# Attention and a gated layer on one core: one left-over sum for two pairs, and another engine for the last piece of key weights

## The chip, the cores and the metric

The kernel runs on one core of one Trainium2 chip. The metric is the device time of one execution in microseconds, the median of several runs. The core has five engines that work from queues of their own: TensorE (PE, matmuls; its weight loads are PEld), VectorE (DVE), ScalarE (ACT), GpSimd (POOL) and SyncE (SP, which here only starts DMA transfers). Each works strictly in the order in which the program gave it its instructions.

## The reference, cut to what matters

```python
# q, k, v: (8 batches, 12 heads, 448 rows, 64)
scores = cap * np.tanh(scale * (q @ k.T) / cap)
attn = np.exp(scores - max); attn = attn / (attn.sum(-1) + 1e-9)
x = (attn @ v) as (8, 448, 768)
xk = mu_k * x + (1 - mu_k) * x_prev          # x_prev: x one row earlier
xr = mu_r * x + (1 - mu_r) * x_prev
k = np.maximum(xk @ w_k, 0)                   # 768 -> 1024
out = sigmoid(xr @ w_r) * (k * k @ w_v)
```

All is float32. Products that need more than one pass are made of a high and a low part of each operand. The weights come as float64 and are put together from their two 32-bit words on the chip.

## The kernel before, in words

**Pairs and steps.** The 8 x 12 heads are 48 pairs of two heads. `run` calls `step(i)` once per pair; each step is a string of operations written out by hand (lines 59 to 82), and `step` (L840) calls them one after the other. So the strings fix the order of the work on every engine. A number in a name is a group of keys: 448 keys are three groups of 128 (0, 1, 2) and 64 left-over keys. Group 3 holds the left-over keys of two pairs, i and i + 1, together: at even steps `S3` (scores), `tanh3` and `exp3` work on one tile of 128 x 2 x 448 for both pairs, whose index 1 is i % 2 (with the 128 partitions shared by two heads).

**The sums of a pair.** `red` (L345) sums exponentials over 32 keys at a time on VectorE with a transposing reduce. For groups 0 to 2 it reads 128 x 896 and writes 128 x 28; for group 3 it reads one pair's half of the tile, 128 x 448, and writes 128 x 14. So there is a `red3` at every step: at even steps behind `exp3`, near the step's end, and at odd steps ahead of the `f`s. The results lie in `r1` (L182), one for even and one for odd pairs, each the first row of a tile `sq_0` or `sq_1`. In the next step `gather` (L353) moves partitions 32 to 127 of `r1` to partitions 0 to 31 with three DMAs of SP's queue; `recip` (L357, four VectorE instructions) adds them up, inverts and transposes; `rec_store` writes the reciprocals to DRAM, and `rec_load` (L372, two DMAs on SP's queue) reads them back spread over 128 partitions as `r`. In the step after that `norm` (L381, VectorE) multiplies the pair's values, in PSUM as `pv`, by `r`. `mix_old` (L392, ACT) and `mix_new` (L394, VectorE) mix rows; `mix_new` is the last to read the pair's `pv` bank, of which there are two, and so lets `V`, the product of exponentials and values of a later pair (L314 and L340), begin. `x_high` and `x_low` (GpSimd) split the mixed rows.

**Key weights.** The pieces of w_k are made in steps 0 to 12: piece n is loaded in step n - 1, `weight_abs` takes its magnitude in step n, and five calls of `f` (`fill`, each one a step of the generator `weight_round`) do one VectorE instruction each (L577, L580, L582, L584, L586). `weight_sum` (L591) then adds the two words (L593), copies the sum as its high part to `wkh` (L122) and subtracts to get the low part `wkl` (L132), all three on GpSimd. Pieces 10 and 11 are halves, 384 columns wide, of the last 128 of the 1024 key columns. Piece 11 gets its five `f`s in step 12, and `weight_sum` follows in the same step. The matmuls with the key weights (`K`, six at a time here, L474) of step 12 are the last 18 of batch 0: they need both pieces, the last nine of them piece 11, and they stand one behind the other in PE's queue.

**Step 12.** Its string (`TURN[0]`, L80) is, with what each engine sees of it cut to this case:

```
... S0 S1 V S3 S2 f f f f f gate_new tanh0 exp0 red0 norm
weight_sum tanh1 exp1 K relu_early red1 tanh3 tanh2 qk_high ... mix_new recip ... qk_low x_high x_low ...
K red2 ... K relu k_store weight_abs exp3 red3 ... load_qk rec_load weight_store N0 N1
```

The `norm` of step 12 is that of pair 10, and its `r` is loaded behind the end of step 11. `qk_high` and `qk_low` are GpSimd work (L122, L132) on a later pair. From step 13 on the matmuls of the next batch (L498) fill PE; after step 47 the second half of the kernel multiplies by w_v and w_r (L711).

Of the kernel before, what the change touches and what calls it, by code (L numbers as in the profile page):

```python
# [10 lines left out]
F32 = mybir.dt.float32  # L11
F32R = mybir.dt.float32r
AF = mybir.ActivationFunctionType
ALU = mybir.AluOpType
# [15 lines left out]
P = 128  # L30
# [18 lines left out]
RM = 3 * NB  # L49
RC = RM + NB // 2  # L50
# [5 lines left out]

ODD = """load_v gather quad_load weight_load S0 S1 V S2 red3 f f f f f gate_new tanh0 exp0 red0
weight_sum tanh1 exp1 red1 norm recip x_store rec_store K qk_high qk_low tanh2 relu mix_old k_store prep mix_new x_high x_low gate_old  # L60
K exp2 red2 weight_rest weight_sum relu k_store prep K prep K relu k_store prep
weight_abs load_qk rec_load quad_load tail_open weight_store"""
EVEN = ODD.replace("V S2", "V S3 S2").replace(" red3", "").replace("tanh2", "tanh3 tanh2").replace("K relu k_store prep\n", "K exp3 red3 relu k_store prep\n")
ROWS = """gather weight_store load_v quad_load quad_load weight_load 135:U 3:turn PE 135:red3 f f f f f tanh0 exp0 0:turn 0:PE_TURN red0
weight_sum tanh1 15:PE_TURN exp1 23:relu red1 gate_new norm recip x_store 1:k_put rec_store 235:k_put qk_high qk_low 024:tanh3 tanh2 0234:exp2 4:turn mix_old mix_new x_high x_low gate_old
15:exp2 red2 weight_rest weight_sum 0:weight_abs 0:relu 024:exp3 024:red3 12345:weight_abs load_qk rec_load PE_END"""
ROWS_PE = (("VV S3 S2", "K18", "N0 N1"), ("K15", "S2 N0 turn K15", "N1"), ("WW K6 T S3 S2 K18", "", "N0 N1"),
# [1 line left out]
STEP_0 = """gather rec_load load_v x_store weight_load S0 S1 V0 S2 V1 S3 V2 V3 f f f f f tanh0 exp0 red0  # L69
weight_sum tanh1 exp1 weight_abs red1 recip rec_store qk_high qk_low tanh2 exp2 norm red2 tanh3 exp3 mix_old red3 mix_new x_high x_low  # L70
load_qk weight_store"""
ODD_6 = """load_v gather weight_load weight_low S0 S1 V S2 red3 f f f f f gate_new tanh0 exp0 red0 norm
weight_sum tanh1 exp1 K relu_early red1 tanh2 qk_rise relu exp2 mix_old k_store mix_new recip x_store rec_store qk_low x_high x_low gate_old
K red2 weight_rest weight_sum relu k_store K K weight_abs relu k_store load_qk rec_load weight_store"""
EVEN_6 = ODD_6.replace("V S2", "V S3 S2").replace(" red3", "").replace("tanh2 qk_rise", "tanh3 tanh2 qk_high").replace("weight_abs", "weight_abs exp3 red3")
STEP_6 = """gather rec_load load_v x_store weight_load weight_low S0 S1 V0 S2 V1 S3 V2 V3 f f f f f tanh0 exp0 red0
weight_sum tanh1 exp1 red1 recip rec_store tanh2 qk_rise exp2 norm red2 K qk_low weight_abs tanh3 exp3 mix_old red3 mix_new x_high x_low
load_qk rec_load"""
STEP_1 = STEP_0.replace("S3 ", "").replace("tanh3 exp3 mix_old red3", "mix_old").replace("f f f f f", "red3 f f f f f")
TURN = (EVEN_6.replace("K K weight_abs", "K relu k_store weight_abs") + " N0 N1",  # L80
        " ".join(x for x in ODD_6.replace("S0 S1 V S2", "U K15").replace("tanh1", "tanh1 S2 N0 turn K15").split() if x not in ("K", "relu", "relu_early", "k_store")) + " N1")
LAST = """gather f f f f VV recip rec_store norm rec_load K mix_old relu k_store prep mix_new x_high x_low gate_old
K gate_new relu k_store prep K prep K relu k_store prep x_store tail_open"""
# [4 lines left out]
def rows(phase):  # L88
    pe = dict(zip(("PE", "PE_TURN", "PE_END"), ROWS_PE[phase]))
    do = [x.split(":") for x in ROWS.split()]  # L90
    return " ".join(pe.get(x[-1], x[-1]) for x in do if len(x) == 1 or str(phase) in x[0])


def strings(i):
    if i < ALONE:
        return ((STEP_0, STEP_1) if i < 6 else (STEP_6, ODD_6))[i % 2]
    if i < REST[0]:
        return (TURN if i >= 12 else (EVEN_6, ODD_6))[i % 2]
    if i < NPAIR:
        return rows(i % NP)  # L100
    return ((LAST.replace("gather", "gather relu k_store"), LAST) if i < NPAIR + 2 else (EVEN, ODD))[i % 2]


def f(ap):
    return ap.bitcast(F32)


class Body:
# [73 lines left out]
    def init_sums(self, pool):  # L182


        nc = self.nc
        self.r1, self.sr, self.sq = [], [], []
        for j in range(2):
            t = pool.tile([P, 8, RC], F32, name=f"sq_{j}")
            self.r1.append(t[:, 0])
            self.sq.append(t[0:32])  # L190
            self.sr.append(pool.tile([32, 32], F32, name=f"sr_{j}"))
            nc.gpsimd.memset(self.sr[j], 1.0)

# [151 lines left out]
    def red(self, i, g):  # L345
        p32, r1 = self.P32[i, g], self.r1[i % 2]
        if g == 3:
            p32 = p32[:, i % 2:i % 2 + 1]
        self.nc.vector.tensor_reduce(out=r1[:, 0:RM].rearrange("p (x g) -> p x g", g=3)[:, :, g] if g < 3 else r1[:, RM:RC],  # L349
                                     in_=p32.rearrange("p h (b k) -> p (h b) k", k=32),  # L350
                                     axis=mybir.AxisListType.X, op=ALU.add, apply_transpose=True)

    def gather(self, i):  # L353
        for q in range(1, 4):
# [236 lines left out]
    def weight_sum(self, e="p"):  # L591
        for n, a, sq in self.w_sum:
            {"p": self.nc.gpsimd, "v": self.nc.vector}[e].tensor_add(sq, f(a), sq)  # L593
            cols = self.key_piece(n)
            if cols:
                c, d = cols
                hi, lo = (x[:, d[0]:d[-1] + 1, c * P:(c + 1) * P] for x in (self.WKH, self.WKL))
                sq = sq.rearrange("p (c n) -> p c n", n=P)
                self.copy(e, hi, sq)
                if len(d) < ND:  # L600
                    self.sub(e, lo, sq, f(hi))
                else:
                    self.w_low.append((lo, sq, hi))
            else:
                self.w_done.append((n, sq))
        self.w_sum = []

    def weight_low(self):
        for lo, sq, hi in self.w_low:
            self.sub("v", lo, sq, f(hi))  # L610
        self.w_low = []
# [469 lines left out]
```

## Time and profile before

| | |
|---|---|
| median of 3 runs | 889.12 us (887.44 to 890.73) |
| the profiled execution | 889.26 us, its span 887.4 us |
| PE busy | 862.9 us (97%) |
| DVE, ACT, POOL busy | 730.0, 624.8, 411.1 us |
| mean granted TensorE clock | 0.99 |

The span runs from the first to the last instruction; the 1.9 us between it and the execution's own time lie around it. PE's busy time is modelled, since matmuls overlap. In what follows a time such as 127.11 is in us from the start of the span.

### The profile page before, as it was taken

The page shows a single profiled execution, that of the slowest core. Times are in us where ns is not written, and L with a number is a line of the kernel's source. Part 1 is how long each engine was busy: PE and PEld are TensorE (multiplying, and loading weights), DVE is VectorE, ACT ScalarE, POOL GpSimd, SP SyncE. Part 2 cuts the span into 40 slices and gives each one's busy share as a digit, 9 for nine tenths or more (in the row PEclk, how much of TensorE's full clock was granted, in tenths as well). Part 3 has the DMA queues.
Part 4 walks back from the last instruction along what each step waited for, and adds up shares of the span by engine and source line. Part 5 has one row for each costly group of instructions (what it writes and reads, how often), then busy time and mean ns, then how long its engine had stood idle before and what let it go on. Part 6 is the DMA issues. An engine that isn't in the chain of part 4 may idle for free.

```text
span 887.4 us, 16618 instructions
## 1 busy us (share of the span) xinstructions
PE 862.9 (97%) x5826; PEld 707.7 (80%) x5826; DVE 730.0 (82%) x1246; ACT 624.8 (70%) x922; POOL 411.1 (46%) x346
## 2 busy tenths in 40 slices
PE   7789999999999999999999999999999999999996
PEld 3226667777766777777766899999999999999996
DVE  6988996999999999999879847888787667777775
ACT  8897888988888889888786655665656535555553
POOL 4996584777877777867754100000000033333430
PEclk9889999999999999999999999999999999999999
DMA  5575746577676667666665738554546546667763
GB/s 162 168 215 183 215 144 197 183 207 227 201 225 210 202 201 232 209 215 186 189 215 180 242 107 259 162 173 145 168 150 182 159 136 209 218 216 215 219 216 103
DMA packets 121374, 169.53 MB, mean 191 GB/s; under 512 B 20288, under 2 KB 105408, under 8 KB 121280
## 3 DMA queue, kind: packets, MB, share of 16 engines
q1 hardware_dynamic: 118544, 164.04, 59.5%
q10 hardware_dynamic: 2736, 4.33, 1.3%
q8 instruction: 48, 0.79, 0.4%
q14 instruction: 46, 0.38, 0.2%
HBM read 109.91 MB, written 56.60 MB: 188 GB/s over the span
## 4 chain that ended last, share of the span: by engine, by line
PE 88%; DVE 5%; ACT 1%; POOL 1%; DMA 1%; issue 1%; SPq 1%; ACTq 0%; DVEq 0%; POOLq 0%
PE ps L711 40%; PE kps L498 19%; PE pv L314 11%; PE s L277 9%; PE kps L474 4%; PE pv L340 2%; PE s L270 2%; DVE sq L349 2%; PE s L474 1%; ACT p L290 1%; ACT p L303 1%; DVE wa L582 0%; DVE xk L397 0%; DVE wa L580 0%; DMA sq<-sq 0%
## 5 line engine op out<-in xcount | busy, mean ns | idle before, releaser
L349 DVE TRANSPOSE_TENSOR_REDUCE sq<-p 128x28 f32<-128x896 f32 (+1 forms) x192 | 181.1, 971 | 17.1 <-ACT p L303 17.1
L290 ACT ACTIVATE p<-s,scl_t 128x896 f32<-128x896 f32 x168 | 165.5, 997 | 27.9 <-PE s L270 22.3
L303 ACT ACTIVATE p<-p,cap_t 128x896 f32<-128x896 f32 x168 | 175.1, 1042 | 4.3 <-ACT ko L510 0.4
L675 POOL TENSOR_TENSOR s<-src 128x384 f32<-128x384 f32 x14 | 14.3, 1020 | 264.5 <-DVE lo L696 264.5
L711 PE MATMUL ps<-wvh,hi 128*128 128x384 f32 x392 | 131.0, 334 | 0.0
L711 PE MATMUL ps<-wvl,hi 128*128 128x384 f32 x392 | 131.0, 334 | 0.0
L314 PE MATMUL pv<-p,rv 128*64 128x448 f32 x576 | 120.6, 560 | 8.8 <-DVE xk L397 8.7
L695 ACT CAST hi<-s 128x512 fp32r<-128x512 f32 (+1 forms) x112 | 63.6, 567 | 90.3 <-PE ps L711 75.7
L696 DVE TENSOR_TENSOR lo<-s,hi 128x512 fp32r<-128x512 f32 (+1 forms) x112 | 70.8, 632 | 59.7 <-ACT hi L695 43.9
L132 POOL TENSOR_TENSOR qkl<-rqk,qkh 128x896 fp32r<-128x896 f32 x47 | 109.3, 2326 | 8.3 <-ACT qkh L126 4.8
L498 PE MATMUL kps<-xkh,wkh 64*128 64x448 f32 (+1 forms) x540 | 110.0, 367 | 0.0
L498 PE MATMUL kps<-xkl,wkh 64*128 64x448 f32 (+1 forms) x540 | 109.3, 362 | 0.0
L498 PE MATMUL kps<-xkh,wkl 64*128 64x448 f32 (+1 forms) x540 | 109.0, 361 | 0.0
L711 PE MATMUL ps<-wrh,hi 128*128 128x384 f32 x294 | 98.9, 336 | 0.3 <-DVE o L734 0.3
L711 PE MATMUL ps<-wrl,hi 128*128 128x384 f32 x294 | 98.8, 336 | 0.0
L314 PEld LDWEIGHTS pv<-p,rv 128*64 128x64 f32 x576 | 38.4, 139 | 72.9 <-issue 50.0
L695 ACT CAST hi<-src 128x512 fp32r<-128x512 f32 (+1 forms) x84 | 47.7, 568 | 62.4 <-PE ps L711 59.5
L711 PE MATMUL ps<-wvh,lo 128*128 128x384 f32 x392 | 83.7, 334 | 0.0
L696 DVE TENSOR_TENSOR lo<-src,hi 128x512 fp32r<-128x512 f32 (+1 forms) x84 | 56.9, 678 | 21.1 <-ACT hi L695 19.2
L711 PEld LDWEIGHTS ps<-wvh,hi 128*128 128x128 f32 x392 | 73.6, 188 | 0.1
L711 PEld LDWEIGHTS ps<-wvl,hi 128*128 128x128 f32 x392 | 73.6, 188 | 0.0
L593 POOL TENSOR_TENSOR wsq<-wa,wsq 128x384 f32<-128x384 f32 (+1 forms) x40 | 43.9, 1097 | 63.1 <-DVE wsq L586 60.8
(118 smaller groups left out, 1920.2 us busy)
## 6 DMA issues: line engine op xcount, KB each, us to landing
rqk<-qk SPq DMA_DIRECT2D x47, 448.0 KB
src<-k_d SPq DMA_DIRECT2D x56, 256.0 KB
rv<-v SPq DMA_DIRECT2D x48, 256.0 KB
r<-rec_d SPq DMA_DIRECT2D x96, 112.0 KB
v_d<-o SPq DMA_DIRECT2D x56, 192.0 KB
src<-x_d SPq DMA_DIRECT2D x42, 256.0 KB
vl<-v_d SPq DMA_DIRECT2D x56, 192.0 KB
out<-o SPq DMA_DIRECT2D x55, 192.0 KB
```

The source lines that it names most:

```text
L132: {"p": self.nc.gpsimd, "v": self.nc.vector}[e].tensor_sub(*a)
L277: nc.tensor.matmul(s[:, (h + i) % 2, 0:S], qk[a][p, k], qk[b][p, 0:S], start=(n == 0), stop=(n == 2))
L290: self.nc.scalar.activation(p32[:, n], self.S.pop((i, g))[:, n, 0:S], AF.Tanh, scale=self.scl_t)
L303: self.nc.scalar.activation(p32, p32, AF.Exp, scale=1.0 if self.maxima else self.cap_t)
L314: nc.tensor.matmul(pv[p, 0:S], v[:, g, h, :], ph[:, (h + i) % 2, :], start=(g == 0), stop=False)
L349: self.nc.vector.tensor_reduce(out=r1[:, 0:RM].rearrange("p (x g) -> p x g", g=3)[:, :, g] if g < 3 else r1[:, RM:RC], in_=p32.rearrange(" ...
L474: nc.tensor.matmul(self.kps[fc][:, 0:S], w, m[:, dc, :], start=first, stop=last)
L498: self.nc.tensor.matmul(self.kps[c][:, 0:S], w[p, dc, c * P:(c + 1) * P], m[p, dc, :], start=s == 0, stop=last or way == 2 and t == 2, ski ...
L593: {"p": self.nc.gpsimd, "v": self.nc.vector}[e].tensor_add(sq, f(a), sq)
L695: self.nc.scalar.copy(hi, x)
L696: self.nc.vector.tensor_sub(lo, x, f(hi))
L711: self.nc.tensor.matmul(o, a[:, c, :], w[:, c, :], start=first and k == 0, stop=last and k == len(todo) - 1, skip_group_check=True)
```

## The change

The tiles `sq_0` and `sq_1` become one tile of 128 x 2 x 8 x 98 with a view `left_sums` of the 14 left-over columns of both pairs. `red` for group 3 sums both pairs' left-over keys in one VectorE instruction at the even step, 128 x 896 in and 128 x 28 out, and the odd steps have no `red3`. In step 12 `weight_last` takes the place of the first `weight_sum`: the same add, copy and subtraction, on VectorE.

```diff
-ODD = """... S0 S1 V S2 red3 f f f f f gate_new tanh0 exp0 red0
+ODD = """... S0 S1 V S2 f f f f f gate_new tanh0 exp0 red0
...
-EVEN = ODD.replace("V S2", "V S3 S2").replace(" red3", "")...
+EVEN = ODD.replace("V S2", "V S3 S2")...
...
-ROWS = """... PE 135:red3 f f f f f tanh0 ...
+ROWS = """... PE f f f f f tanh0 ...
...
-STEP_1 = STEP_0.replace("S3 ", "").replace("tanh3 exp3 mix_old red3", "mix_old").replace("f f f f f", "red3 f f f f f")
-TURN = (EVEN_6.replace("K K weight_abs", "K relu k_store weight_abs") + " N0 N1",
+STEP_1 = STEP_0.replace("S3 ", "").replace("tanh3 exp3 mix_old red3", "mix_old")
+TURN = (EVEN_6.replace("K K weight_abs", "K relu k_store weight_abs").replace("weight_sum tanh1", "weight_last tanh1") + " N0 N1",
...
+        t = pool.tile([P, 2, 8, RC], F32, name="sq_")
+        self.left_sums = t[:, :, 0, RM:RC]
         for j in range(2):
-            t = pool.tile([P, 8, RC], F32, name=f"sq_{j}")
-            self.r1.append(t[:, 0])
-            self.sq.append(t[0:32])
+            self.r1.append(t[:, j, 0])
+            self.sq.append(t[0:32, j])
...
         if g == 3:
-            p32 = p32[:, i % 2:i % 2 + 1]
-        self.nc.vector.tensor_reduce(out=r1[:, 0:RM]... if g < 3 else r1[:, RM:RC],
-                                     in_=p32.rearrange("p h (b k) -> p (h b) k", k=32),
-                                     axis=mybir.AxisListType.X, op=ALU.add, apply_transpose=True)
+            out, p32 = self.left_sums, p32.rearrange("p j (b k) -> p j b k", k=32)
+        else:
+            out, p32 = r1[:, 0:RM]..., p32.rearrange("p h (b k) -> p (h b) k", k=32)
+        self.nc.vector.tensor_reduce(out=out, in_=p32, axis=mybir.AxisListType.X, op=ALU.add, apply_transpose=True)
...
+    def weight_last(self):
+        self.weight_sum("v")
```

## Rows read from the trace of the kernel before

**Rows 1.** Busy time by stretch: from:to, length, PE (instructions), granted clock, DMA, GB/s.

```profile
57.00:64.00 7.00, 6.33 (x22) 0.51 0.77 243
...
32.00:36.50 4.50, 4.33 (x14) 0.50 0.22 74
...
133.00:480.00 347.00, 346.97 (x2926) 1.00 0.66 206
```

**Rows 2.** The same view of all engines: PE, PEld, DVE, ACT, POOL, PEclk.

```profile
60.00:80.00 20.00, 20.00 (x108) 10.78 (x106) 17.92 (x29) 16.84 (x20) 15.94 (x14) 0.90 0.63 189
...
100.00:120.00 20.00, 19.41 (x112) 12.94 (x112) 19.52 (x31) 17.30 (x21) 14.61 (x12) 1.00 0.56 167
```

**Rows 3.** The chain that ended last, around step 12's key weights: start, us, what.

```profile
126.63 0.57 DVE wsq L586
...
127.27 1.02 POOL wsq L593
...
128.97 1.00 POOL wkl L132
...
130.01 1.89 PE kps L474 x8
```

**Rows 4.** Timeline of VectorE in step 12: start, us, instruction, idle time before.

```profile
124.42 1.19 DVE L580 TENSOR_SCALAR wa<-wsq 128x384 uint32<-128x384 uint32 x1
...
126.24 0.36 DVE L584 TENSOR_SCALAR wsq<-wa 128x384 uint32<-128x384 uint32 x1
...
127.11 1.11 DVE L349 TRANSPOSE_TENSOR_REDUCE sq<-p 128x28 f32<-128x896 f32 x1
129.69 0.63 DVE L382 TENSOR_TENSOR x<-pv,r 128x448 f32<-128x448 f32 x1 [1.47 <-DMA r<-rec_d]
130.23 1.10 DVE L349 TRANSPOSE_TENSOR_REDUCE sq<-p 128x28 f32<-128x896 f32 x1
```

**Rows 5.** Timeline of TensorE in step 12.

```profile
128.44 0.36 PE L474 MATMUL kps<-xkl,wkh 128*128 128x448 f32 x1
128.94 0.47 PE L474 MATMUL kps<-xkh,wkh 128*128 128x448 f32 x1
130.01 0.47 PE L474 MATMUL kps<-xkh,wkl 128*128 128x448 f32 x1 [0.61 <-POOL wkl L132]
```

**Rows 6.** Timeline of SP's queue in steps 11 and 12.

```profile
123.18 0.34 SPq L369 DMA_DIRECT2D rec_d<-rs  x1
...
125.70 1.12 SPq L378 DMA_DIRECT2D r<-rec_d  x2
```

**Rows 7.** Timeline of VectorE in steps 9 to 13: sums and what starts behind them.

```profile
98.88 1.09 DVE L349 TRANSPOSE_TENSOR_REDUCE sq<-p 128x28 f32<-128x896 f32 x1
99.90 0.64 DVE L397 SCALAR_TENSOR_TENSOR xk<-x,mu_k,pv 128x448 f32<-128x448 f32 x1
...
114.98 0.62 DVE L349 TRANSPOSE_TENSOR_REDUCE sq<-p 128x14 f32<-128x448 f32 x1
115.54 0.30 DVE L577 TENSOR_SCALAR wsq<-wsq 128x384 f32<-128x384 f32 x1
```

**Rows 8.** Timeline of VectorE around step 15, with PE full.

```profile
153.48 2.15 DVE L349 TRANSPOSE_TENSOR_REDUCE sq<-p 128x28 f32<-128x896 f32 x3
...
161.69 0.49 DVE L359 TENSOR_REDUCE sq<-sq 32x28 f32<-32x336 f32 x1
```

**Rows 9.** Timeline of GpSimd in steps 11 and 12.

```profile
124.15 1.25 POOL L132 TENSOR_TENSOR xkl<-xk,xkh 128x448 fp32r<-128x448 f32 x1
...
130.95 2.12 POOL L132 TENSOR_TENSOR qkl<-rqk,qkh 128x896 fp32r<-128x896 f32 x1
```

**Rows 10.** Timeline of TensorE: its three longest waits after the kernel's start.

```profile
32.17 1.01 PE L314 MATMUL pv<-p,rv 128*64 128x448 f32 x2 [3.15 <-DVE xk L397]
...
49.20 0.60 PE L314 MATMUL pv<-p,rv 128*64 128x448 f32 x2 [1.53 <-DVE xk L397]
...
57.67 1.01 PE L314 MATMUL pv<-p,rv 128*64 128x448 f32 x2 [2.72 <-DVE xk L397]
```

More of the change, by code (lines that the diff above doesn't have):

```diff
@@ L52 @@
 LATE = [*range(12), NPAIR - 2, NPAIR - 1]
-ODD = """load_v gather quad_load weight_load S0 S1 V S2 red3 f f f f f gate_new tanh0 exp0 red0
+ODD = """load_v gather quad_load weight_load S0 S1 V S2 f f f f f gate_new tanh0 exp0 red0
 weight_sum tanh1 exp1 red1 norm recip x_store rec_store K qk_high qk_low tanh2 relu mix_old k_store prep mix_new x_high x_low gate_old
@@ L62 @@
 weight_abs load_qk rec_load quad_load tail_open weight_store"""
-EVEN = ODD.replace("V S2", "V S3 S2").replace(" red3", "").replace("tanh2", "tanh3 tanh2").replace("K relu k_store prep\n", "K exp3 red3 relu k_store prep\n")
-ROWS = """gather weight_store load_v quad_load quad_load weight_load 135:U 3:turn PE 135:red3 f f f f f tanh0 exp0 0:turn 0:PE_TURN red0
+EVEN = ODD.replace("V S2", "V S3 S2").replace("tanh2", "tanh3 tanh2").replace("K relu k_store prep\n", "K exp3 red3 relu k_store prep\n")
+ROWS = """gather weight_store load_v quad_load quad_load weight_load 135:U 3:turn PE f f f f f tanh0 exp0 0:turn 0:PE_TURN red0
 weight_sum tanh1 15:PE_TURN exp1 23:relu red1 gate_new norm recip x_store 1:k_put rec_store 235:k_put qk_high qk_low 024:tanh3 tanh2 0234:exp2 4:turn mix_old mix_new x_high x_low gate_old
@@ L71 @@
 load_qk weight_store"""
-ODD_6 = """load_v gather weight_load weight_low S0 S1 V S2 red3 f f f f f gate_new tanh0 exp0 red0 norm
+ODD_6 = """load_v gather weight_load weight_low S0 S1 V S2 f f f f f gate_new tanh0 exp0 red0 norm
 weight_sum tanh1 exp1 K relu_early red1 tanh2 qk_rise relu exp2 mix_old k_store mix_new recip x_store rec_store qk_low x_high x_low gate_old
 K red2 weight_rest weight_sum relu k_store K K weight_abs relu k_store load_qk rec_load weight_store"""
-EVEN_6 = ODD_6.replace("V S2", "V S3 S2").replace(" red3", "").replace("tanh2 qk_rise", "tanh3 tanh2 qk_high").replace("weight_abs", "weight_abs exp3 red3")
+EVEN_6 = ODD_6.replace("V S2", "V S3 S2").replace("tanh2 qk_rise", "tanh3 tanh2 qk_high").replace("weight_abs", "weight_abs exp3 red3")
 STEP_6 = """gather rec_load load_v x_store weight_load weight_low S0 S1 V0 S2 V1 S3 V2 V3 f f f f f tanh0 exp0 red0
@@ L347, in red @@
         if g == 3:
-            p32 = p32[:, i % 2:i % 2 + 1]
-        self.nc.vector.tensor_reduce(out=r1[:, 0:RM].rearrange("p (x g) -> p x g", g=3)[:, :, g] if g < 3 else r1[:, RM:RC],
-                                     in_=p32.rearrange("p h (b k) -> p (h b) k", k=32),
-                                     axis=mybir.AxisListType.X, op=ALU.add, apply_transpose=True)
+            out, p32 = self.left_sums, p32.rearrange("p j (b k) -> p j b k", k=32)
+        else:
+            out, p32 = r1[:, 0:RM].rearrange("p (x g) -> p x g", g=3)[:, :, g], p32.rearrange("p h (b k) -> p (h b) k", k=32)
+        self.nc.vector.tensor_reduce(out=out, in_=p32, axis=mybir.AxisListType.X, op=ALU.add, apply_transpose=True)
     def gather(self, i):
```

## The prediction

> **What bounds the kernel now.** I read the busy time by stretch first. From 133 us on TensorE is full: 346.97 of 347 us at clock 1.00 [rows 1], and nothing that another engine gains there can move the end. What counts is when TensorE gets there: a microsecond lost or won before 133 us is lost or won at the end. Before that TensorE is not the only bound. Its three longest waits after the start all end with `mix_new` on VectorE, the instruction that frees a `pv` bank [rows 10]; from 60 to 80 us TensorE is full, and from 100 to 120 us VectorE is busy for 19.52 of 20 us beside TensorE's 19.41 [rows 2]. Then comes the chain of waits. Around step 12 it leaves VectorE with the last of piece 11's five instructions, passes through GpSimd's add, copy and subtraction, and enters TensorE at 130.01 [rows 3]. TensorE's own timeline shows the cost: a matmul starts at 128.44, the next at 128.94 (it waited for the high part) and the one after at 130.01 (for the low part) [rows 5]. At some 0.2 us from start to start the two would have begun at 128.64 and 128.84; 1.17 us are lost. That is all that the second edit can win.
>
> **The merged sum.** It removes 48 sums of 128 x 448 and adds 24 of 128 x 896 in their place, which are of the size of the other groups' sums. From start to next start a large one takes 99.90 - 98.88 = 1.02 us, a small one 115.54 - 114.98 = 0.56 [rows 7]: a couple of pairs saves 2 x 0.56 - 1.02 = 0.10 us. Six couples (pairs 0 to 11) lie before step 12's weights, so 0.6 us at most, if VectorE were the bound throughout. It is not: what is saved before 60 us must pass through the stretch in which TensorE is full [rows 2], and at even steps up to 6 the longer sum stands ahead of `mix_new`, which it delays by 1.02 - 0.56 = 0.46 us, for GpSimd, ScalarE and TensorE to wait on. The couples of steps 8 and 10 come later, and their 0.2 us count. I take 0.2, with -0.4 and 0.6 as ends. In the full part the saving is worth nothing. The even pair's `gather` starts 0.46 us later there; its cover is the time from the sums at 153.48 to `recip` at 161.69 [rows 8], far more than 0.46. If that cover were gone, `recip` and `norm` would be late by up to 0.46 us a couple. There is a new order to keep, since the even step's sum now writes the odd pair's columns, which the previous `gather` reads: that transfer is issued at the start of the same step and the sum ends it, and in steps of 10 us this costs nothing. SP's queue keeps its order and its number of DMAs. The single tile has the same bytes, and the two pairs' halves lie apart in it.
>
> **The last piece.** `weight_sum` and `tanh1` stand on two sides of a blank in step 12's string, so the replacement hits, and the five `f`s of that step have just put piece 11, and it alone, on the list. Three instructions leave GpSimd (from 127.27 to 129.97, ready for TensorE at 130.01 [rows 3]) and three are added to VectorE. Their prices: an add of two 384-wide operands as L586's 0.57 [rows 3], so about 0.60 to the start of what depends on it; the copy as the 384-wide one-operand instruction, 0.36 busy and 0.39 to the next start [rows 3, 4]; the subtraction 0.56. Together 1.55 us against GpSimd's 2.70. But place decides. In VectorE's queue they stand behind `red0` and behind `norm`, because the string has `red0 norm` ahead of them. `norm` of pair 10 began at 129.69, after 1.47 us of idle time, when `r` landed [rows 4]. Behind it is queued what GpSimd did in its own time before. So: 129.69, plus 130.23 - 129.69 = 0.54 for `norm` [rows 4], plus 1.55, plus the 0.04 us that the hand-over took, makes 131.82 where it was 130.01. TensorE starts again 1.81 us later, less the 0.2 won before (the reciprocals of pair 10, stored at 123.18, follow VectorE, and the loads at 125.70 follow that store [rows 6]): **1.6 us lost**. Would `norm` be less late? Its data came 6.5 us after the store's issue, `red0` ends about 5 us after it, so I see no way without a faster transfer. Lower end: `norm` right behind `red0`, at 127.11 + 1.02 = 128.13 [rows 4, 7], gives 130.26, a loss of 0.25 - 0.2 = 0.05. Upper end: the copy takes 1.19 instead of 0.36, as the one-operand instruction at 124.42 did [rows 4], 2.4 us.
>
> That instruction ran while GpSimd worked on `xkl` from 124.15 [rows 9]; its equal at 126.24 had GpSimd idle. The Trainium skill (SBUF — State Buffer, Who interferes with whom) says that the two engines share a pair of ports under an exclusive lock which such copies can take; by that rule, if GpSimd is at work when `weight_last` copies, the sum grows by the 0.8 us of the upper end. I leave it out of the sum, since GpSimd, rid of three instructions, has only pair 14's casts (the longer one 2.12 us [rows 9]) to do from 125.4 on and then itself waits for `mix_new`, which stands behind `weight_last`.
>
> Behind `weight_last` on VectorE wait `red1`, `mix_new` and `recip`, 1.55 us more; with TensorE later by about as much, their readers are not early, and I add nothing.
>
> **The clock.** The wait in TensorE grows from two short ones to a gap from 128.64 to about 131.2, 2.6 us, one matmul, and another half microsecond. After gaps of 2.72 and 3.15 us the next matmuls took 1.01 us and the granted clock was 0.50 (that is 1.2 GHz, half of 2.4); after one of 1.53 us they took 0.60 [rows 1, 10]. The new gap is nearer to the first two. What it costs: from 32 to 36.5 TensorE worked 4.33 us at 0.50, so it lost half of that, 2.2 us; from 57 to 64 it worked 6.33 at 0.51 and lost 3.1 [rows 1]. The ends are 0 and 3.1; I take 2.2, the lesser of the two prices paid, since a matmul falls into the new gap. Everything behind is TensorE's own work, so all of it reaches the end.
>
> **The sum.** 1.6 + 2.2 = 3.8 us more: 889.26 becomes 893.1 in the profiled execution, and on the median of 889.12, which lies 0.14 below it, **892.9**.
>
> **The rivals.**
> The clock holds: the gap is short of 2.72, and a matmul interrupts it. Then 889.12 + 1.6 = 890.7. For it speaks the wait of 1.53 us without a fall, against it that both longer ones fell. Chance 0.22.
> The low clock lasts (the other side of the bound): TensorE stays at half for as long as from 57 to 64 us. Then 1.6 + 3.1 = 4.7, 893.8. It decides from a price of 4.45 - 1.6 = 2.85 us on, within what the trace shows, and a slow copy would push the same way. Chance 0.20.
> `norm` is not late, since `r` lands by 128: the three instructions end where GpSimd's did, and only 0.05 us are lost, 889.2. Against it: 6.5 us from store to landing. Chance 0.08.
> The clock turns early: in step 5 the longer sum delays `mix_new`, the gap of 1.53 us before 49.20 becomes about 2, the clock falls there, where TensorE has time, and is back at 57.67, where it was low before [rows 10]. That gives back up to 3.1 of the 3.8: 889.8. Chance 0.03.
> The forecast keeps 0.47.
>
> **How the numbers follow.** A measurement of this kernel can tell about 0.5% from no change, 4.45 us: 884.7 to 893.6. The forecast lies inside by 0.7 us only, so slower by more gets the 0.20 of the long low clock and a sliver of the forecast's upper side, 0.21. No sum comes near a gain of 4.45: 1.17 us of wait, 0.6 of sums and 3.1 of clock would all have to go right; 0.02. Within: 0.77. The range goes from between the cases without a fall of the clock, 889.8, to the long low clock with some of the slow copy, 894.7; it leaves out mainly the case of the timely `norm`.
>
> **What would show it.** Right: in step 12 TensorE's `kps` wait names VectorE and ends near 131.6; VectorE's add starts behind `norm` near 130; a stretch of 0.50 in the granted clock begins between 129 and 133 and lasts over 4 us; 24 sums of 128 x 28 in place of 48 of 128 x 14, and full TensorE from 137 us on. Wrong: `norm` without idle time before it, no such stretch of clock, or a change of TensorE's waits before 60 us by more than half a microsecond.

## The result and the profile after

The changed kernel takes **896.57 us** (median of 5 runs, 892.32 to 898.11) against 888.79 us of the kernel before beside it (5 runs, 887.43 to 890.73): ratio 1.0074, 95% interval 1.0057 to 1.0092. A second set of five runs on another occasion gave 894.47 against 889.52, ratio 1.0053 (1.0039 to 1.0066). The change makes the kernel slower by 0.5 to 0.7%; the forecast was 892.9, with a range up to 894.7. The profiled execution of the changed kernel is the quickest of its first five, 892.32 us with a span of 890.5.

The page's busy times and its costliest group first.

```profile
span 890.5 us, 16594 instructions
...
PE 862.5 (97%) x5826; PEld 708.2 (80%) x5826; DVE 731.1 (82%) x1225; ACT 624.8 (70%) x922; POOL 409.4 (46%) x343
...
L352 DVE TRANSPOSE_TENSOR_REDUCE sq__195<-p 128x28 f32<-128x896 f32 x168 | 179.4, 1092 | 18.1 <-ACT p L304 18.1
```

All 168 sums are large ones now, at the same 1092 ns, and no engine works noticeably more or less. So the microseconds are mostly waiting time. The view of busy time by stretch (from:to, length, then PE, PEld, DVE, ACT and POOL with their instructions, granted clock, DMA share, GB/s) says where:

```profile
57.00:64.00 7.00, 6.85 (x38) 2.65 (x40) 5.77 (x12) 6.94 (x9) 6.58 (x8) 1.00 0.71 233
...
127.50:130.98 3.48, 0.01 (x1) 0.00 (x1) 3.38 (x7) 0.98 (x2) 0.03 (x1) 0.97 0.40 145
130.98:134.30 3.32, 3.32 (x9) 2.73 (x9) 3.22 (x7) 0.00 (x0) 1.02 (x2) 0.52 0.00 0
...
133.00:480.00 347.00, 347.00 (x2918) 253.34 (x2918) 308.78 (x505) 289.92 (x372) 245.03 (x195) 1.00 0.65 205
```

From 127.50 to 130.98 TensorE does nothing while VectorE is busy throughout, and in the 3.32 us behind it the granted clock is 0.52, that is close to 1.2 GHz, the lower of its two levels, instead of 2.4. From there on TensorE is as full as before [rows 1]. TensorE's timeline around the gap, the counterpart of [rows 5]:

```profile
127.15 0.36 PE L475 MATMUL kps<-xkl,wkh 128*128 128x448 f32 x1
130.98 0.74 PE L475 MATMUL kps<-xkh,wkh 128*128 128x448 f32 x1 [3.47 <-DVE wkh L124]
131.57 0.74 PE L475 MATMUL kps<-xkh,wkl 128*128 128x448 f32 x1
```

From the ninth key product to the second that needs piece 11 (I call this **the stall** from here on) it takes 131.57 - 127.15 = 4.42 us; before, 130.01 - 128.44 = 1.57 [rows 5]. Why 2.85 us more? VectorE's timeline, the counterpart of [rows 4]:

```profile
123.13 1.19 DVE L581 TENSOR_SCALAR wa<-wsq 128x384 uint32<-128x384 uint32 x1
124.35 1.18 DVE L583 SCALAR_TENSOR_TENSOR wa<-w,wa 128x384 uint32<-128x384 uint32 x1
125.57 2.18 DVE L585 TENSOR_SCALAR wsq<-wa 128x384 uint32<-128x384 uint32 x1
127.78 0.56 DVE L587 SCALAR_TENSOR_TENSOR wsq<-w,wsq 128x384 f32<-128x384 uint32 x1
128.26 1.11 DVE L352 TRANSPOSE_TENSOR_REDUCE sq__195<-p 128x28 f32<-128x896 f32 x1
129.29 0.59 DVE L383 TENSOR_TENSOR x<-pv,r 128x448 f32<-128x448 f32 x1
129.80 0.54 DVE L594 TENSOR_TENSOR wsq<-wa,wsq 128x384 f32<-128x384 f32 x1
130.37 0.55 DVE L124 CAST wkh<-wsq 128x384 fp32r<-128x384 f32 x1
130.96 0.56 DVE L132 TENSOR_TENSOR wkl<-wsq,wkh 128x384 fp32r<-128x384 f32 x1
```

The three new instructions stand behind `norm`, as forecast. But `norm` waits for nothing: VectorE comes late to it, since its third instruction for piece 11 took 1.18 us and its fourth 2.18, where the fourth took 0.36 before [rows 4]. GpSimd's timeline, the counterpart of [rows 9], has the cause beside it:

```profile
122.86 1.24 POOL L132 TENSOR_TENSOR xkl<-xk,xkh 128x448 fp32r<-128x448 f32 x1
124.06 1.07 POOL L122 TENSOR_SCALAR qkh<-rqk 128x896 fp32r<-128x896 f32 x1
125.22 2.31 POOL L132 TENSOR_TENSOR qkl<-rqk,qkh 128x896 fp32r<-128x896 f32 x1
133.19 0.56 POOL L122 TENSOR_SCALAR xkh<-xk 128x448 fp32r<-128x448 f32 x1 [5.66 <-DVE xk L398]
```

Pair 14's copy and subtraction stood behind piece 11's sum in GpSimd's queue, the subtraction at 130.95 [rows 9]. With the sum gone from that queue they run at once, at 124.06 and 125.22, beside the instructions of VectorE that make piece 11. VectorE's 2.18 us end 0.22 us behind GpSimd's subtraction. The Trainium skill (SBUF — State Buffer, Who interferes with whom) has it that VectorE and GpSimd arbitrate for one pair of ports, that one holds it for a whole instruction and the other is blocked meanwhile, also where VectorE's instruction has two inputs; the rows agree, with 1.18 for 0.56 and 2.18 for 0.36. Only the end comes a little early: an instruction of 0.36 us that was blocked to the end of GpSimd's subtraction would end 0.36 us behind it and not 0.22. The 0.36 of the kernel before stands in [rows 4], the 0.56 is this row of it:

```profile
125.64 0.56 DVE L582 SCALAR_TENSOR_TENSOR wa<-w,wa 128x384 uint32<-128x384 uint32 x1
```

The chain of waits (start, us, what) closes the account, against [rows 3]:

```profile
126.17 2.39 DMA sq__195<-sq__195
128.57 0.00 DVEq L383
128.57 0.72 issue
129.29 0.59 DVE x L383
129.88 0.47 DVE wsq L594
130.35 0.02 issue
130.37 0.56 DVE wkh L124
...
130.98 3.67 PE kps L475 x9
```

By 128.57 VectorE's queue (DVEq) has nothing more to wait for ahead of `norm`. The row names the transfer of `gather`, which `norm` does not read: it reads `pv` and `r`, and `r`'s two loads stand ahead of the `gather` in SP's queue, issued at 124.33 and 124.86; the marks of their landings in the trace end at 128.43. `norm` starts 0.72 us after 128.57, because `red0` is late. From there the hand-over runs through VectorE alone.

### The profile page after: what moved, and what is told of

It reads as the page before. It is cut to its first block, busy times and chain, and to the rows that moved or that the text cites. A ratio compares the mean times of both kernels' runs of the same rounds, so it can differ in the third digit from the quotient of the medians.

```text
span 890.5 us, 16594 instructions
## 1 busy us (share of the span) xinstructions
PE 862.5 (97%) x5826; PEld 708.2 (80%) x5826; DVE 731.1 (82%) x1225; ACT 624.8 (70%) x922; POOL 409.4 (46%) x343
## 4 chain that ended last, share of the span: by engine, by line
PE 82%; DVE 7%; ACT 4%; DMA 3%; issue 1%; SPq 1%; POOL 0%; ACTq 0%; DVEq 0%
PE ps L715 40%; PE kps L499 18%; PE pv L315 9%; PE s L278 8%; PE kps L475 3%; DVE sq__195 L352 2%; DMA sq__195<-sq__195 2%; ACT p L291 2%; PE pv L341 2%; ACT p L304 2%; PE s L271 1%; PE s L475 1%; DVE x L383 1%; DVE xk L398 1%; SPq L356 1%
## 5 line engine op out<-in xcount | busy, mean ns | idle before, releaser
L352 DVE TRANSPOSE_TENSOR_REDUCE sq__195<-p 128x28 f32<-128x896 f32 x168 | 179.4, 1092 | 18.1 <-ACT p L304 18.1
L715 PEld LDWEIGHTS ps<-wvh,lo 128*128 128x128 f32 x392 | 69.4, 188 | 0.0
```

Source lines behind the costliest of these rows:

```text
L352: self.nc.vector.tensor_reduce(out=out, in_=p32, axis=mybir.AxisListType.X, op=ALU.add, apply_transpose=True)
L715: self.nc.tensor.matmul(o, a[:, c, :], w[:, c, :], start=first and k == 0, stop=last and k == len(todo) - 1, skip_group_check=True)
```

## The experiments

Each kernel ran in 5 rounds (5 to 12 runs) beside the kernel before. Besides the median, each table has three times from the trace: the stall; from its end to the values of step 13 (the `pv` matmuls at 141.36 in the kernel before and 144.12 after); and from the values of step 12 (121.84 and 120.56) to those of step 13, here **the stretch**. It leaves out what differs from execution to execution ahead of step 12 and in the kernel's last part. That is not little: over the traces of this study step 12's values start between 120.23 and 124.60 us, and from step 13's values to the end of the span it takes 746.0 to 748.6 us.

| kernel | stall | rest | stretch | median against before |
|---|---|---|---|---|
| before | 1.57 | 11.35 | 19.52 | |
| changed | 4.42 | 12.55 | 23.56 | +7.8, 1.0074 |

### The two edits apart, and GpSimd's casts

The merged sums alone (the changed kernel with GpSimd on piece 11's sum):

```diff
-...replace("weight_sum tanh1", "weight_last tanh1") + " N0 N1",
+... + " N0 N1",
```

> The merged sums alone, with step 12's key weights on GpSimd as before. If the second edit costs all of the time (theory of the place), this is no slower than the kernel before: 887 to 889.5 us, TensorE at step 12's second kps matmul at about 128.7 (1.3 us early, as the changed kernel's TensorE was at 120.56 against 121.84). If the merged sums cost (theory of the sums: the longer sum delays mix_new in steps 2 to 6 and moves the stretches of low clock), it is slower by 2 to 6 us and spreads as the changed kernel's runs do (892.3 to 898.1).

The last piece on VectorE alone (the kernel before with `weight_last`):

```diff
-        ... + " N0 N1",
+        ....replace("weight_sum tanh1", "weight_last tanh1") + " N0 N1",
```

> VectorE makes the last half piece, the sums are as before. Theory of the place: slower by 3 to 7 us (892 to 896), with VectorE's instructions of 0.56 and 0.36 us in step 12 stretched by GpSimd's casts to 1 to 2 us, TensorE waiting some 3.5 us and a stretch of clock 0.50 behind it. Theory of the sums: within 1.5 us of the kernel before.

The changed kernel once more, as a measure for the others:

> The changed kernel once more, for a second trace and for its spread: 892 to 898 us, median near 896. If the spread is the clock's, the runs' times go with their low-clock stretches, 0.5 us of time per 1 us at 0.50; if it is the collision of VectorE and GpSimd in step 12, the stretched instructions there differ from those of the first trace (1.18 and 2.18 us).

And the changed kernel with pair 14's casts behind pair 10's splits in GpSimd's queue:

```diff
+ .replace("qk_high ", "").replace("qk_low x_high x_low", "x_high x_low qk_high qk_low")
```

> The changed kernel with pair 14's two casts in step 12 put behind pair 10's two splits in GpSimd's queue, so that GpSimd has nothing to do while VectorE makes the last half piece. Theory that the collision costs: L583 and L585 of step 12 back at 0.56 and 0.36 us, norm waiting for r again (some 0.4 us of idle time), the low part ready about 0.9 us earlier, and 1 to 4 us faster than the changed kernel, the more if the low clock goes. Theory that only the place behind norm costs: within 0.5 us of the changed kernel.

| kernel | stall | rest | stretch | median against before |
|---|---|---|---|---|
| sums alone | 1.60 | 11.30 | 19.48 | +0.7, 1.0005 (0.9996 to 1.0014) |
| last piece alone | 4.41 | 13.62 | 24.63 | +5.2, 1.0050 (1.0033 to 1.0068) |
| changed, again | 4.41 | 12.66 | 23.67 | +5.0, 1.0053 (1.0039 to 1.0066) |
| casts late | 3.90 | 12.65 | 23.15 | +4.5, 1.0049 (1.0036 to 1.0062) |

The second edit does the harm, alone as well as together with the first. Its price has two parts that the table keeps apart. The stall grows by 2.84 to 2.85 us. The rest grows by 1.2 to 2.3, and that is the low clock: in the stretch 130.98 to 134.30 above, most of the nine products start 0.37 us or more apart, where in the kernel before they start 0.20 apart.

With the casts late, VectorE's timeline in step 12 reads:

```profile
125.26 0.36 DVE L585 TENSOR_SCALAR wsq<-wa 128x384 uint32<-128x384 uint32 x1
...
129.03 0.63 DVE L383 TENSOR_TENSOR x<-pv,r 128x448 f32<-128x448 f32 x1 [1.79 <-DMA sq__195<-sq__195]
...
130.15 0.55 DVE L124 CAST wkh<-wsq 128x384 fp32r<-128x384 f32 x1
```

The 0.36 is back and the collision is gone, but `norm` waits 1.79 us for the transfer (the row names the `gather` again; the marks of `r`'s landings end at 128.84), and the stall is only 0.52 us shorter. Of the some 2.4 us by which GpSimd slowed VectorE (1.18 and 2.18 for 0.56 and 0.36), the wait for `r` hid all but half a microsecond here. The half microsecond is that execution's, since it depends on when `r` lands. In the seven traces with the casts in the change's place and the last piece behind `norm`, `norm` starts 2.09 to 2.14 us after the ninth key product, while the landing marks of `r` lie 0.63 to 1.83 us after it; a VectorE that is ready starts `norm` 0.19 us after landing (in the kernel before and in others). So VectorE comes last in all seven, by 0.1 us (the changed kernel again) to 1.3. The place behind `norm` is the larger cost (with the casts late the stall is 3.90 against 1.57), and the collision comes on top of it, by more the sooner `r` lands.

### Other places, and small matmuls in the gap

Two kernels put `weight_last` ahead of `norm`: right behind the `f`s, or behind `red0`, both with the casts late. A third has it behind the `f`s with the casts in the change's place. In all three `weight_last` is gone from its place behind `norm`; the replacements for the late casts are left out here.

```diff
+ ... .replace("f gate_new", "f weight_last gate_new") ...      # behind the f's
...
+ ... .replace("red0 norm", "red0 weight_last norm") ...        # behind red0
```

> VectorE makes the last half piece right behind its five instructions, ahead of red0 and norm, and pair 14's casts stand behind pair 10's splits on GpSimd. If the place behind norm and the casts are the whole cost, TensorE's wait between the ninth kps matmul of step 12 and the second one that needs piece 11 (3.9 to 4.4 us from start to start in the changed kernels, 1.57 before) falls to about 0.6, no clock of 0.50 follows, and the kernel is about 1 us faster than before: 888 to 889. If VectorE is the wrong engine in itself (its 1.7 us delay red0, norm and mix_new), it stays at or above the kernel before by over 1 us.

> The same place ahead of red0 and norm, but with pair 14's casts where the change left them. The casts then stretch VectorE's instructions (1.2 and 2.2 us) with nothing to hide that: the low part is ready some 1.9 us later than without them, 2.5 to 3 us from the ninth kps matmul to the second that needs piece 11, and 1.5 to 4 us slower than the one with late casts (by more where the clock falls). If the collision is harmless, the two are within 0.7 us.

> The last half piece between red0 and norm, with late casts: against the kernel with late casts alone only the order of norm and the last piece differs. If the wait for r in front of norm is what costs, 1.5 to 1.7 us from the ninth kps matmul to the second that needs piece 11, as before the change, no low clock, and 888.5 to 890.5 us, 3.5 to 5 us faster than the kernel with late casts. If not, within 1 us of that kernel.

The fourth is the changed kernel with 24 matmuls of 64 columns behind the ninth key product. They change the sum of the last 128 key columns of batch 0.

```diff
+            if (b, fc, dc, t) == (0, NF - 1, 2, 2):
+                for _ in range(24):
+                    nc.tensor.matmul(self.kps[fc][:, S:512], w, m[:, dc, 0:512 - S], start=True, ...)
```

> The changed kernel with 24 small matmuls (64 columns, on columns that nobody reads) put where TensorE waits in step 12, so that the wait is as long but not idle. If the low clock behind the wait is a cost of its own, the granted clock stays at 1.00 after 128 us and the kernel is 1.6 to 3 us faster than the changed kernel (891 to 893), still 2.5 to 3 us slower than the one before. If the clock costs nothing, within 0.7 us of the changed kernel.

| kernel | stall | rest | stretch | median against before |
|---|---|---|---|---|
| behind the `f`s, casts late | 0.58 | 12.56 | 19.74 | +2.0, 1.0015 (1.0004 to 1.0025) |
| behind the `f`s | 2.99 | 11.44 | 21.03 | +3.4, 1.0031 (1.0019 to 1.0042) |
| behind `red0`, casts late | 1.43 | 11.44 | 19.47 | +1.7, 1.0016 (1.0005 to 1.0027) |
| changed, small matmuls | 4.39 | 12.72 | 23.71 | +6.2, 1.0063 (1.0049 to 1.0076) |

Ahead of `norm`, with the casts late, nearly everything in the stretch is regained: it is that of the kernel before to within 0.2 us. So VectorE can do the work in the time, and what the change costs there depends on the place in its queue. The medians do not come back as far: +2.0 and +1.7 are clear of noise, 890.55 where 888 to 889 was expected and 890.29 within the 888.5 to 890.5 expected, and the stretch does not show what they hold. Behind the `f`s the stall even falls to 0.58, a whole microsecond below that of the kernel before, and the stretch does not. TensorE's timeline in step 13 shows where it went:

```profile
136.47 0.47 PE L278 MATMUL s<-qkh 64*128 64x448 f32 x2 [0.23 <-ACT turned L506]
...
137.51 0.47 PE L278 MATMUL s<-qkh,qkl 64*128 64x448 f32 x2 [0.56 <-POOL qkl L132]
```

The casts put off are now late for the scores of pair 14 (0.56 us for their low part), and the scores wait 0.23 us for `turned` as well, a one-column copy of ScalarE's. With the casts early the collision costs its full price here, since nothing behind the `f`s waits for a transfer that could hide it: the stall is 2.99, 2.4 us more.

The small matmuls filled most of the gap (another 0.84 us of idle time is left behind them) and did not help. The same view of busy time by stretch:

```profile
131.40:134.20 2.80, 2.76 (x25) 2.65 (x23) 2.77 (x5) 0.74 (x2) 0.15 (x1) 1.00 0.49 177
135.00:139.00 4.00, 4.00 (x11) 2.89 (x13) 3.90 (x8) 0.12 (x1) 1.71 (x2) 0.57 0.00 0
```

TensorE was busy for 2.76 of 2.80 us, and the clock was near its lower level behind it all the same, where I had expected it to stay at 1.00.

### Work in the gap

The scores of pair 13 (`N0 N1`, two groups, 1.34 us of TensorE, at the end of step 12) need nothing that step 12 makes. Three kernels have them behind the ninth key product: the changed one, the merged sums alone, and the kernel before.

```diff
- ... + " N0 N1",
+ ... .replace("K red2", "K3 N0 N1 K3 red2"),
```

> The changed kernel, with the two groups of scores of pair 13 (1.34 us of TensorE, at the end of step 12 so far) moved into the wait, behind the ninth product of the keys. Theory (the loss is TensorE's idle time in step 12 and the low clock behind it): VectorE delivers piece 11 as late as before, so TensorE is idle 1.34 us less, and the rest of the gap is 3.47 - 1.34 = 2.1 us. 3.1 us over the kernel before if the clock stays full (5.0 measured for the changed kernel less 1.3, less a part of the 1.65 to 3.1 of clock), 3.7 over it if the clock still falls. Rival 1 (the loss comes from elsewhere: the early steps, or what GpSimd and VectorE hand on later than before): no change against the changed kernel, 4.9 to 5.9 over the kernel before. Rival 2 (VectorE is what is late, and TensorE's order costs nothing): step 13 gives the 1.34 us back, as it did with the late casts, and the time is as the changed kernel's.

> The merged sums alone, with GpSimd on the last half piece's sum as in the kernel before, and the two score groups of pair 13 in the wait. The wait for piece 11 was 0.78 to 1.2 us there and the scores take 1.34 us. Theory (TensorE's order is the critical path from step 12 on): the wait goes, and the time falls by about 1.0 us, to 0.5 to 1.0 us under the kernel before, ratio 0.9985 to 0.9995: a version faster than both, if only just measurable. Rival (ScalarE or VectorE is late by then and TensorE's 1.0 us is given back in step 13): no difference from the kernel with the merged sums alone, 0.0 to 0.8 us over the kernel before.

> The kernel before, with the two score groups of pair 13 in the wait for piece 11 (1.57 us from the ninth product to the second that needs the piece, some 1.1 us of it idle). Theory (TensorE's order bounds the time from step 12 on, and the merged sums are worth nothing): 0.8 to 1.1 us under the kernel before, ratio 0.9988 to 0.9991, and within 0.5 us of the kernel with the merged sums and the scores early. Rival 1 (the wait's 1.1 us is given back in step 13): ratio 1.000. Rival 2 (the merged sums do help once the wait is gone): the kernel with them is 0.2 us or more under this one.

The fourth separates the clock from the stall, with matmuls of full width that nobody reads.

```diff
+            if (b, fc, dc, t) == (0, NF - 1, 2, 2):
+                spare = self.ps_s.tile([P, 2, 512], F32, name="s")
+                for n in range(14):
+                    nc.tensor.matmul(spare[:, n % 2, 0:S], w, m[:, dc, :], start=True, stop=True)
```

> The changed kernel, with 14 products of 448 columns (0.21 us each at full clock, 2.9 us in all) into a spare score buffer in the wait, behind the ninth product; nobody reads them. TensorE waits for piece 11 as late as in the changed kernel (4.4 us from the ninth product to the second that needs the piece), with 0.6 us or less of it idle. It tells the stall from the clock. Theory (of the 5.0 to 5.9 us lost, 2.85 are stall and 1.65 to 3.1 the low clock behind it): the granted clock is full at 131 us, and the time is 2.5 to 3.2 us over the kernel before. Rival 1 (the clock falls all the same, as behind 24 products of 64 columns): 0.5 until some 135 us, 4.9 to 5.9 us over the kernel before. Rival 2 (the clock's low stretch is only moved to a later one): full at 131 us, the time as the changed kernel's, and a low stretch elsewhere.

| kernel | stall | rest | stretch | median against before |
|---|---|---|---|---|
| changed, scores early | 4.38 | 12.54 | 23.53 | +6.4, 1.0058 (1.0044 to 1.0072) |
| sums alone, scores early | 2.02 | 11.18 | 19.80 | +1.8, 1.0018 (1.0001 to 1.0034) |
| before, scores early | 2.03 | 11.23 | 19.84 | +1.1, 1.0007 (0.9995 to 1.0020) |
| changed, wide matmuls | 4.40 | 11.35 | 22.35 | +4.9, 1.0051 (1.0033 to 1.0069) |

My theory fell in the first three. TensorE's idle time did shrink by about what the scores take (2.00 instead of 3.47 us), and the changed kernel's stretch is the same; in the two others it is 0.3 us longer. TensorE's timeline of the changed kernel with the scores early:

```profile
131.78 0.74 PE L475 MATMUL kps<-xkh,wkh 128*128 128x448 f32 x1 [2.00 <-DVE wkh L124]
...
136.11 0.47 PE L499 MATMUL kps<-xkh,wkh 64*128 64x448 f32 x1 [0.24 <-ACT ko L511]
...
140.42 0.47 PE L278 MATMUL s<-qkh 64*128 64x448 f32 x2 [0.41 <-ACT turned L506]
```

Two waits for ScalarE have taken the place. ScalarE's own timeline has the first and the last link of what they wait for:

```profile
135.51 0.54 ACT L511 ACTIVATE ko<-kps 128x448 f32<-128x448 f32 x1 [4.16 <-PE kps L475]
...
140.27 0.15 ACT L506 COPY turned<-kps 128x1 f32<-128x1 f32 x1
```

From the last key product on, ScalarE does the ReLU of the keys, the issue of their store, an exponential, two tanhs with an exponential between them, and the copy `turned`, for which the next scores wait: 140.27 - 135.51 = 4.76 us, in the kernel before as here. In the usual order TensorE has the two score groups and 30 products to do in that time, and finishes just as ScalarE does. Without the scores there it arrives early and waits. So the end of piece 11 counts through two paths at once, and work put ahead of it shortens only one.

The wide matmuls answer the other question. The busy time by stretch behind the gap:

```profile
132.00:136.00 4.00, 3.88 (x27) 3.12 (x28) 3.90 (x8) 1.33 (x2) 1.72 (x2) 1.00 0.08 30
```

The clock is 1.00 and the rest is 11.35 us, what it was in the kernel before, with the stall as long as ever. The filling matmuls leave 0.61 us of idle time. So in the profile the low clock costs 12.55 - 11.35 = 1.2 us, and the stall its 2.85. The median does not follow: +4.9, where 2.5 to 3.2 us were expected, is no lower than the +5.0 of the changed kernel's second set.

### Both paths at once

If two paths are tied, both must be shortened. The exponential of the left-over keys can leave ScalarE's chain: in the kernel before ScalarE is idle for 1.24 us ahead of `mix_old`.

```diff
+ .replace("exp2 mix_old", "exp2 exp3 mix_old").replace("weight_abs exp3 red3", "weight_abs red3")
```

> The changed kernel with the scores of pair 13 in the wait, as in the run before that gained nothing, and with ScalarE's exponential of the left-over keys (1.05 us) moved from behind the ReLU of the keys to ahead of the mix, where ScalarE is idle. Theory (the stall's end is tied twice: TensorE's own order, and ScalarE's chain from the last key product over the ReLU, the exponential, the tanhs and the copy `turned`, 4.76 us in every kernel): the chain is 3.7 us, TensorE's wait for `turned` goes, the wait for the ReLU's buffer (0.5 us) stays; from the values of step 12 to those of step 13 it takes 22.5 to 22.9 us instead of 23.5, and the time is 0.6 to 1.0 us under that of the kernel with the scores alone. Rival (what TensorE gains is lost somewhere further on, whatever ScalarE does): 23.5 us and no difference.

> The kernel before with both moves: the scores of pair 13 in its wait for piece 11 and the exponential of the left-over keys ahead of the mix. Theory (TensorE's order and ScalarE's chain bound step 12 together, so that each move alone gains nothing and both together do): from the values of step 12 to those of step 13 it takes 18.8 to 19.1 us instead of 19.5, and the time is 0.4 to 0.7 us under the kernel before, ratio 0.9992 to 0.9996. Rival (no such tie, or a third one at the same place): 1.0 us over, as with the scores alone.

> The same two moves on the kernel with the merged sums and GpSimd on the last half piece. Theory (the merged sums are worth nothing): within 0.5 us of the kernel before with both moves, 18.8 to 19.1 us from values to values. Rival (the merged sums gain once nothing waits in step 12): 0.2 us or more under it; or they cost, as the 0.8 us between the two kernels with the scores alone could be read: 0.5 us or more over it.

> The kernel before with the exponential alone moved ahead of the mix. Theory (in the kernel before TensorE reaches the scores behind `turned` just as ScalarE is done with it; a shorter chain on ScalarE alone leaves TensorE's own order as the bound): 19.5 us from values to values and a ratio of 1.000. Rival (ScalarE's chain alone is the bound of step 12, and TensorE's order has slack): 18.5 to 18.9 us, 0.6 to 1.0 us under the kernel before.

| kernel | stall | rest | stretch | median against before |
|---|---|---|---|---|
| changed, both moves | 4.39 | 12.19 | 23.18 | +4.4, 1.0043 (1.0027 to 1.0059) |
| before, both moves | 2.01 | 10.56 | 19.17 | -0.5, 0.9997 (0.9986 to 1.0008) |
| sums alone, both moves | 2.02 | 10.62 | 19.23 | +1.0, 1.0008 (0.9996 to 1.0021) |
| before, exponential alone | 1.58 | 11.20 | 19.38 | -0.8, 0.9992 (0.9980 to 1.0004) |

The tie shows in single traces, smaller than I had said; two traces of the changed kernel differ by 0.11 us in the stretch. The scores alone lengthen the stretch of the kernel before by 0.32 us, the exponential alone shortens it by 0.14, and the two together by 0.35, just outside the 0.4 to 0.7 that were expected. In the changed kernel both moves bring the stretch from 23.53 to 23.18, and not to the 22.5 to 22.9 expected. ScalarE's chain, in the kernel before with both moves:

```profile
131.98 0.54 ACT L510 ACTIVATE ko<-kps 128x448 f32<-128x448 f32 x1 [0.81 <-PE kps L474]
...
135.93 0.16 ACT L505 COPY turned<-kps 128x1 f32<-128x1 f32 x1
```

It is 3.95 us long, where I expected 3.7, and TensorE's wait for the ReLU's buffer stays:

```profile
132.58 0.47 PE L498 MATMUL kps<-xkh,wkh 64*128 64x448 f32 x1 [0.23 <-ACT ko L510]
```

With the exponential alone it is ScalarE that waits for TensorE, so TensorE's own order is then the longer path:

```profile
134.81 0.16 ACT L505 COPY turned<-kps 128x1 f32<-128x1 f32 x1 [0.55 <-PE kps L498]
```

Neither kernel is faster than the kernel before by more than the measurement can tell. No version in this study beats it measurably.

## Why the prediction was wrong, and what was right

**The direction and the place** were right. The wait names VectorE, and the low clock follows it. That the second product starts at 131.57, close to the forecast 131.6, is luck: TensorE came to step 12 earlier by 1.28 us and its stall was longer than forecast by 1.24. The low clock lasted 3.3 us, not the over 4 of the forecast. The merged sums are worth nothing in the stretch (19.48 against 19.52 us), with 0.2 predicted. TensorE came to step 12 earlier in the first trace of the changed kernel, 120.56 against 121.84, and the case of a clock that turns early did show there: TensorE's three waits, against [rows 10],

```profile
31.76 1.76 PE L315 MATMUL pv<-p,rv 128*64 128x448 f32 x4 [2.10 <-DVE xk L398]
...
48.71 1.66 PE L315 MATMUL pv<-p,rv 128*64 128x448 f32 x4 [1.90 <-DVE xk L398]
...
57.15 0.97 PE L315 MATMUL pv<-p,rv 128*64 128x448 f32 x4 [1.14 <-DVE xk L398]
```

have the longer gap and the long matmuls ahead of 48.71 and a full clock at 57.15, as that rival had it. That two of these waits changed by more than half a microsecond, 2.72 to 1.14 and 3.15 to 2.10, is also a sign of being wrong that the forecast names. No gain is seen from it: the trace of the sums alone has the same pattern (waits of 1.92 and 1.36 us at the two later places) and its step 12's values start at 122.44, later than before, and the median of the sums alone is +0.7 with an interval that includes no change.

**The step that failed is the stall**, a loss put at 1.6 us (1.81 less 0.2) on the premise that VectorE stands ready when `r` lands. It is 2.85. Counted from the ninth key product, `norm` started 1.25 us after it before and 2.14 after the change: 0.89 more, of which about 0.7 is a VectorE that was late and about 0.2 a transfer that landed later (1.28 against 1.06 us after the ninth product). In the second trace of the changed kernel the same delay is 0.1 of VectorE and 0.8 of the transfer: both were close to the end there. From `norm` to the second product it took 2.28 us instead of the 2.13 predicted, mostly because the copy takes 0.55 and not the 0.36 of the row I took for it. The 0.2 us of the sums were no gain. 0.89 + 0.15 + 1.81 = 2.85.

**Why VectorE was late** stands in the prediction as the thing left out: GpSimd "has only pair 14's casts (...) to do from 125.4 on and then itself waits for `mix_new`". I had looked for the collision at the three new instructions. What I missed is that work which leaves a queue lets what stands behind it come forward, and that these casts came forward onto the old instructions for the same piece. The forecast's sign of failure, "`norm` without idle time before it", is what happened. The kernel with the casts late prices it at 0.52 us of the stall; by the landing marks a VectorE in time would have been worth 0.1 to 1.3 us from trace to trace.

**The clock** was sized at 2.2 with ends of 0 and 3.1. Behind the stall it cost 1.2 to 1.3 us in the changed kernel (12.55 and 12.66 against 11.35), 2.3 with the last piece alone, and nothing behind the wide matmuls. The mechanism held; the size depends on how soon the clock comes back.

**The sum** of the forecast, 3.8, is near the 4.0 by which the stretch grew in the trace (23.56 - 19.52), by luck: its stall was too small by 1.25 and its clock too dear by 1.0. With both put right the forecast would be about 893.2, not far from the 892.9 it was. What took the first median to 896.57 is therefore not in the sum at all. The medians grew by 7.8 in the first five runs and by 5.0 in the next, the last piece alone by 5.2 where its stretch has 5.1. What lies beyond the stretch in the others is not settled. One reading is a cost of the merged sums outside it: the kernels that differ in them alone stand 0.7, 0.8 and 1.5 us apart (alone, with the scores early, with both moves), to the disadvantage of the merged sums; but the intervals of each two overlap, and the fourth pair, the last piece alone with 5.2 against the changed kernel's second set with 5.0, has it the other way. Another is a wait far behind the stretch. The prediction took TensorE for full from 133 us on, and its row ends at 480 [rows 1]; between 485 and 491 us TensorE waits for `mix_new` once more, for 0.43 to 0.97 us, in eight of the traces, such as the changed kernel's second:

```profile
489.74 2.48 PE L315 MATMUL pv<-p,rv 128*64 128x448 f32 x12 [0.89 <-DVE xk L398]
```

Six of the eight have the merged sums and two do not, and neither the kernel before nor the changed kernel's first trace has it; so it differs between executions, and what it is worth in a median is not shown. Of the changed kernel's first five runs, which reach from 892.3 to 898.1 where its second five lie within 893.9 and 895.2, no trace shows why they differ.

**The rivals.** "The clock holds" fell with the clock's rows in every trace of the changed kernel. "The low clock lasts" came near in the last piece alone. "`norm` is not late" fell: `r` landed late, as I had said, and VectorE came to it later still.

## What to carry to other kernels

When an instruction leaves an engine's queue, look at what stands behind it there: it comes forward, and may meet work of a neighbour that it never met before. When an instruction joins a queue, its place is its price: with the casts out of the way, the same three instructions lengthened the stretch by 3.6 us behind `norm` and by 0.2 at most ahead of it. Before filling a wait with other work, ask what that work was covering where it stood; if the stall's end feeds two engines, shortening one of the two paths gains nothing.

## What the runs showed of the hardware

- Beside GpSimd's copy and subtraction of 128 x 896, two VectorE instructions of 128 x 384 took 1.17 to 1.19 and 2.16 to 2.18 us instead of 0.56 and 0.36, in eight traces alike; GpSimd's subtraction grew only from 2.12 to 2.30 or 2.31 us.
- A one-input copy of 128 x 384 to the rounded type took 0.55 us on VectorE and 0.51 on GpSimd; the add and the subtraction took 0.54 and 0.56 on VectorE, and 1.0 each on GpSimd. So the move made the add and the subtraction shorter, and the copy not.
- Behind a gap filled with 24 matmuls of 64 columns (TensorE busy for 2.76 of 2.80 us, then 0.84 idle) the granted clock stood at 0.57 in the next 4 us; behind the same gap filled with 14 of 448 columns (busy for 2.94 of 3.50 us, 0.61 idle in it) it was 1.00. What made the difference, no run here shows.
